# A block order at the start of two feed-forward phases, a third weight buffer and an earlier routing stage in an attention and mixture-of-experts kernel

## The chip, the cores and the metric

The kernel runs on one core of a Trainium2 chip. The metric is the device time of one execution in microseconds. The kernel before took 1055.02 us, the median of three runs (1054.81 to 1056.46).

## What is computed

Three layers follow each other. In the reference, cut to what matters:

```python
# 1 attention: 4 batches, 8 heads, 768 positions, head size 64; local window 96, 8 global positions
scores = q @ k^T / 8 + bias;  a = softmax(scores);  x = (a @ v) as 3072 tokens x 512
# 2 routing: all 3072 x 8 logits in falling order, an expert takes 384 tokens at most
logits = x @ w_gate
for idx in argsort(-logits.flatten()):
    tok, e = idx // 8, idx % 8
    if assigned[tok] < 0 and counts[e] < 384: assigned[tok] = e; counts[e] += 1
for e in range(8):
    out[mask] = relu(x[mask] @ w1[e]) @ w2[e]        # 512 -> 1024 -> 512
# 3 one dense layer for all tokens
out = (relu(out @ w_in) ** 2) @ w_out                # 512 -> 2048 -> 512
```

## The kernel before

After the attention, a router finds in eight stages which expert is full next and which 384 tokens it has. As soon as a stage is done, the 384 rows of that expert are gathered from memory (an indirect DMA from GpSimd, three of 128 rows), and TensorE runs two phases on them: phase A is the expert's own two matrices (`phase_a`), phase B the dense layer on the same rows (`phase_b`). The order is A and B of the first expert, A and B of the second, and so on (`SEQ`); experts are counted here from 0.

Every 32-bit matmul operand is held as a high half and a low half, and a product is three matmuls: high with high, high with low, low with high (`mm3`). ScalarE copies the high half, VectorE or GpSimd subtracts it for the low half. The rows' transposed operand x (or, in phase B, y) is `xy`: x[0] the high half, x[1] the low half, each of four pieces of 128 rows by 384 tokens, made piece by piece by `parts`.

Phase A goes over 8 row blocks f of 128 hidden units. A block's first product has 12 matmuls into one PSUM bank (`hg`), then `relu` makes the two halves of the result: ScalarE reads the bank first, VectorE reads it after that. Two blocks later 12 matmuls add the second product into four banks (`y`). Phase B goes over 16 row blocks in the same manner, but its `square` reads the bank once, with ScalarE's relu, and its second product (`outp`, 9 matmuls into three banks `o`) comes one block later. The `hg` banks are two, `pt0` and `pt1`, in turn; the transposes of the next expert's rows (`xpose`) use them too.

The weights of phase A are loaded per block (`loads`), and split by `splits`: two tiles of high halves `wh` by ScalarE (one for each product), two of low halves `wl` by GpSimd. The tiles of the first product have two buffers, so block f+2 is split when block f's matmuls have been issued. In the first expert, phase A's first block already sends its 8 matmuls with x[0] ahead of the 4 with x[1]. The weights of phase B stay on the chip; their second matrix is converted during the first expert (`conv`, with the buffers `ob`, of which two are called `cab0` and `cab1`).

A planner (`Sched`, with the costs in `take`) puts the generators' steps of all engines in one order by modelled times and priorities; a `yield` with a function waits until it is true. The routing stage `routing(1)` starts when the first expert's four x pieces are done. A stage has some preparing operations on VectorE, a transposition on TensorE, a search of eleven rounds on VectorE, and a closing part with short matmuls.

Of the kernel before, what the change touches and what calls it, by code (L numbers as in the profile page):

```python
# [6 lines left out]
FT = mybir.dt.float32  # L7
# [172 lines left out]
FR = mybir.dt.float32r  # L180
# [27 lines left out]
def tags(name, n):  # L208
    return tuple(f"{name}{i}" for i in range(n))
# [290 lines left out]
class Router:  # L500
# [110 lines left out]
    def stage(self, s, wp, ps, idx, eidx):  # L611
# [104 lines left out]
        else:  # L716
# [22 lines left out]
            yield "DVE"  # L739
            V.scalar_tensor_tensor(wv[:, 128:192], pv[:, 192:256], self.half[:, 1:2], wv[:, 128:192], op0=OP.mult, op1=OP.add)  # L740
            yield "DVE"
            for d in range(11):
                n, cur = (4, self.tw0) if d == 0 else (JW, thw)
                for j in range(1, n):
# [231 lines left out]
def ffn(tc, pools, router, ident, xd, wab, wov, wol, out, tail, wih, wil):  # L976
# [59 lines left out]
    def routing(s):  # L1036
        idx[s] = sb.tile([128, 3], I32, "idx", tags("idx", 8))
        eidx[s] = sb.tile([1, 1], I32, "eidx", tags("eidx", 8))

        if s == 1: yield lambda: parted["x", 0] == 4  # L1040
        for r in router.stage(s, wp, rps, idx[s], eidx[s]):
            if r == "e": known.add(s)
            elif r == "idx": done.add(s)
            elif r == "soon": soon.add(s)
            else: yield r
        if s + 1 < NE: S.add(routing(s+1), PR[s+1], -1)
    def first_gather():
# [25 lines left out]
    def splits():  # L1073
        for a in range(8*NE):
            yield lambda: a in raw
            w = raw.pop(a)
            W[a] = []
            for k in range(2):
                c = slice(k*512, k*512+512)
                yield lambda: n["ph"] > a - 2 if k == 0 else n["y"] > a - 4  # L1080
                hi = sb.tile([128, 512], FR, f"wh{k}", (tags("w", 2), tags("w", 7)[4:] + ("craw0",))[k])
                lo = sb.tile([128, 512], FR, f"wl{k}", (tags("w", 4)[2:], tags("w", 10)[7:] + ("craw1",))[k])
                yield ("ACT", [w[:, c]], [hi])
                ACT.copy(hi, w[:, c])
                yield first_gather
                yield ("POOL", [hi], [lo])
                G.tensor_tensor(lo, w[:, c], hi, op=OP.subtract)
                W[a] += [hi, lo]
            n["split"] += 1
    def loads_o():  # L1090
# [50 lines left out]
    def parts(kind, s, kc, v):  # L1141
        d = xy
        yield ("ACT", [v], [d[0][:, kc]])
        ACT.copy(d[0][:, kc], v)
        yield ("DVE", [d[0][:, kc]], [d[1][:, kc]])
        V.tensor_tensor(d[1][:, kc], v, d[0][:, kc], op=OP.subtract)
        parted[kind, s] += 1
        if kind == "y" and s not in kept: n["acc"] -= 1
    def xpose(s, kcs, slots):

        yield lambda: s in gathered
        p = {}
        for i, kc in enumerate(kcs):
            p[kc] = pp.tile([128, 384], FT, "xtp" + slots[i], (slots[i],))
        for k in range(3):
            yield ("PE", [xg[:, k]], [p[kcs[0]]])
            for kc in kcs:
                PE.transpose(p[kc][:, k*128:k*128+128], xg[:, k, kc*128:kc*128+128], ident)
        for kc in kcs: S.add(parts("x", s, kc, p[kc]), 0)
        if kcs[-1] == 3: xposed.add(s)  # L1160
    def mm3(o, sh, sl, mh, ml, first, last):
        yield ("PE", [sh, sl, mh, ml], [o])
        PE.matmul(o, sh, mh, start=first, stop=False)
        PE.matmul(o, sh, ml, start=False, stop=False)
        PE.matmul(o, sl, mh, start=False, stop=last)
    hq, gq = {}, {}
    def relu(a, ph):
        hh, hl = rot("hb", hb)
# [5 lines left out]
    def phase_a(s):  # L1174
        x, (nh, ns) = xy, follows["A", s]
        y = []
        yield lambda: parted["x", s] == 4
        for f in range(10):
            a = s*8 + f
            if f < 8:  # L1180
                yield lambda: len(W.get(a, ())) >= 2
# [59 lines left out]
    def rows_out(s, k, o, end):  # L1241
        ot = xg[:, k]
        e = "ACT" if k == 1 + end else "DVE"
        yield (e, [o], [ot])
        if e == "ACT": ACT.copy(ot, o)
        else: V.tensor_copy(ot, o)
        n["acc"] -= 1
        yield "POOL"
        G.memset(spacer, 0.0)
        st = G.indirect_dma_start(out=out, out_offset=bass.IndirectOffsetOnAxis(ap=idx[s][:, k:k+1], axis=0), in_=ot, in_offset=None)  # L1250
        for q in prevsc: tc.declare_no_dep(st.ins, q.ins, reason="other rows")
        prevsc.append(st)
        scattered[s] += 1
    def phase_b(s):
# [4 lines left out]
        def outp(f, ks=range(3)):  # L1259
# [11 lines left out]
            if 2 in ks:  # L1271
                n["out"] += 1
                WO.pop((s, f))
                gq.pop((s, f))
        for f in range(16):
            wh, wl = wih[f], wil[f]
            pg = pp.tile([128, 384], FT, "hg", tags("pt", 2))
            for kc in range(4):
# [3 lines left out]
            if f == 15:  # L1282
# [7 lines left out]
                for k in () if end else range(3):  # L1290
# [2 lines left out]
                        yield lambda: (s, 15) in gq  # L1293
                        yield from xpose(ns, (2, 3), ("pt0", "pt1"))
                    yield from outp(13+k)
            elif 1 <= f < 14:
                yield from outp(f-1)
    def main():

        yield lambda: 0 in done  # L1300
        warm = pp.tile([128, 512], FT, "warm", ("pt0",))
        for _ in range(NWARM):
            yield ("PE", [wih[0]], [warm])
            PE.matmul(warm, wih[0][:, 0:128], wih[0], start=True, stop=True)
        yield lambda: 0 in gathered
        yield from xpose(0, range(4), ("mi", "s0", "s1", "s2"))
        for h, s in seq:
            yield from (phase_a if h == "A" else phase_b)(s)
    def rows(g):
# [179 lines left out]
```

## Time and profile before

| | |
|---|---|
| median of three runs | 1055.02 us |
| profiled execution | 1056.06 us |
| its span, first to last instruction | 1054.3 us |
| TensorE busy (matmuls) | 1021.0 us, 97% |
| VectorE, ScalarE, GpSimd busy | 666.8, 497.2, 418.3 us |
| mean granted clock of TensorE | 0.985 |

The span is that of the profiled execution, which is one run; the median is of others. Matmuls are pipelined, so the length of one matmul in the profile (0.34 us for 384 columns) is longer than the time until the next one starts. Steps between starts are the better measure.

### The profile page before, as it was taken

The page shows a single profiled execution, that of the slowest core. Times are in us where ns is not written, and L with a number is a line of the kernel's source. Part 1 is how long each engine was busy: PE and PEld are TensorE (multiplying, and loading weights), DVE is VectorE, ACT ScalarE, POOL GpSimd, SP SyncE. Part 2 cuts the span into 40 slices and gives each one's busy share as a digit, 9 for nine tenths or more (in the row PEclk, how much of TensorE's full clock was granted, in tenths as well). Part 3 has the DMA queues.
Part 4 walks back from the last instruction along what each step waited for, and adds up shares of the span by engine and source line. Part 5 has one row for each costly group of instructions (what it writes and reads, how often), then busy time and mean ns, then how long its engine had stood idle before and what let it go on. Part 6 is the DMA issues. An engine that isn't in the chain of part 4 may idle for free.

```text
span 1054.3 us, 18941 instructions
## 1 busy us (share of the span) xinstructions
PE 1021.0 (97%) x6427; PEld 909.2 (86%) x6427; DVE 666.8 (63%) x2665; ACT 497.2 (47%) x1246; POOL 418.3 (40%) x458
## 2 busy tenths in 40 slices
PE   9999996899999999999999999999999999999997
PEld 6777775689889888998899889988998899999986
DVE  6999986799569857985797489559954111121111
ACT  8989995334433443334433433433343444333332
POOL 4756630653565143615261526252633272006001
PEclk9999997899999999999999999999999999999999
DMA  9989953553342133214231523242323243223121
GB/s 334 349 308 362 352 201 121 189 151 111 121 149 91 41 120 120 100 41 160 77 105 40 162 69 110 76 125 71 111 90 110 61 148 112 60 79 103 40 61 60
DMA packets 53041, 139.51 MB, mean 132 GB/s; under 512 B 6224, under 2 KB 6608, under 8 KB 52944
## 3 DMA queue, kind: packets, MB, share of 16 engines
q1 hardware_dynamic: 49104, 125.72, 36.1%
q0 software_dynamic: 3840, 12.59, 3.7%
q8 instruction: 50, 0.82, 0.3%
q14 instruction: 47, 0.39, 0.1%
HBM read 117.31 MB, written 20.97 MB: 131 GB/s over the span
## 4 chain that ended last, share of the span: by engine, by line
PE 78%; DVE 11%; issue 4%; ACT 3%; POOL 1%; DMA 1%; POOLq 0%; SPq 0%; DVEq 0%; ACTq 0%
PE hg L77 33%; PE o L77 23%; PE y L77 8%; DVE r_ge L77 4%; PE pt L321 3%; PE pxpx L337 3%; PE s L294 3%; ACT P L312 2%; PE r_ps L77 2%; DVE r_tc L77 1%; DVE r_th L77 1%; DVE r_pre L77 1%; PE natmi L383 1%; DMA c_xg<-xd,idx 1%; DVE r_fc L77 1%
## 5 line engine op out<-in xcount | busy, mean ns | idle before, releaser
L77 PE MATMUL hg<-c_XT,wi 128*128 128x384 f32 x1536 | 291.9, 338 | 2.2 <-DVE c_XT L77 2.2
L77 PEld LDWEIGHTS hg<-c_XT,wi 128*128 128x128 f32 x1536 | 270.4, 188 | 12.7 <-DVE c_XT L77 3.4
L77 ACT ACTIVATE c_gs<-hg 128x384 f32<-128x384 f32 x128 | 63.0, 492 | 281.5 <-PE hg L77 276.2
L77 POOL TENSOR_TENSOR wl<-c_T,wh 128x512 fp32r<-128x512 f32 x128 | 167.1, 1323 | 44.1 <-ACT wh L77 41.7
L77 DVE TENSOR_SCALAR_CACHE_REDUCE r_ge<-r_wv,r_th 128x192 bf16<-128x192 f32 x420 | 172.5, 411 | 11.7
L77 PE MATMUL hg<-c_XT,wh 128*128 128x384 f32 x512 | 132.0, 339 | 3.0 <-DVE c_XT L77 1.9
L77 ACT CAST wh<-c_T 128x512 fp32r<-128x512 f32 x128 | 75.1, 617 | 59.4 <-DMA c_T<-in_wab 57.7
L77 PEld LDWEIGHTS hg<-c_XT,wh 128*128 128x128 f32 x512 | 92.6, 188 | 6.0 <-DVE c_XT L77 3.7
L77 POOL DMA_INDIRECT out<-c_xg,idx x24 | 23.7, 986 | 183.6 <-DVE c_xg L77 169.0
L312 ACT ACTIVATE P<-ns,nm 128x232 f32<-128x232 f32 (+1 forms) x192 | 90.1, 475 | 13.6 <-DVE nm L304 13.2
L77 PE MATMUL hg<-c_XT,wl 128*128 128x384 f32 x256 | 87.1, 340 | 0.7
L77 POOL TENSOR_TENSOR c_k<-c_q,c_k 128x384 fp32r<-128x384 f32 x24 | 25.0, 1042 | 134.1 <-ACT c_k L77 114.3
L77 PE MATMUL o<-wol,c_k 128*128 128x512 f32 x192 | 76.4, 398 | 0.0
L77 ACT ACTIVATE c_q<-c_gs 128x384 f32<-128x384 f32 x128 | 67.2, 525 | 9.0 <-ACT c_gs L77 0.4
L304 DVE CUSTOM_DVE_ANT_0 ns<-s,T 128x232 f32<-128x232 f32 (+1 forms) x192 | 61.4, 375 | 9.0 <-PE s L294 4.0
L321 PE MATMUL pt<-ident,P 128*128 128x128 f32 x352 | 52.3, 283 | 2.6 <-ACT PT L326 2.3
L321 PEld LDWEIGHTS pt<-ident,P 128*128 128x128 f32 x352 | 37.3, 141 | 20.2 <-ACT PT L326 9.5
L77 PE MATMUL y<-c_k,wh 128*128 128x384 f32 x192 | 54.7, 338 | 0.0
L77 PEld LDWEIGHTS hg<-c_XT,wl 128*128 128x128 f32 x256 | 48.1, 188 | 3.4 <-POOL wl L77 3.3
L326 ACT COPY PT<-pt 128x512 f32<-128x512 f32 (+1 forms) x94 | 50.5, 537 | 0.3 <-PE pt L321 0.3
L77 POOL TENSOR_TENSOR c_v<-c_q,c_k 128x384 fp32r<-128x384 f32 x24 | 24.8, 1033 | 62.3 <-ACT c_k L77 48.7
L294 PE MATMUL s<-kr,qr 64*128 64x232 f32 (+1 forms) x384 | 48.6, 372 | 0.0
(304 smaller groups left out, 2087.9 us busy)
## 6 DMA issues: line engine op xcount, KB each, us to landing
c_T<-in_wab SPq DMA_DIRECT2D x64, 512.0 KB, 3.5
wol<-wol SPq DMA_DIRECT2D x128, 256.0 KB, 2.6
raw<-in_m SPq DMA_DIRECT2D x32, 512.0 KB, 7.9
vr<-in_v SPq DMA_DIRECT2D x16, 704.0 KB, 5.7
xd<-xn SPq DMA_DIRECT2D x24, 256.0 KB, 4.0
kr<-in_k SPq DMA_DIRECT2D x15, 404.0 KB, 7.3
qr<-in_q SPq DMA_DIRECT2D x15, 384.0 KB, 7.1
wov<-ct SPq DMA_DIRECT2D x16, 256.0 KB, 6.3
```

What stands on the lines that cost most here:

```text
L77: return f(*a, **k)
L294: PE.matmul(s[a][:, :n], qr[h, i*128:i*128+128], kr[h, c0:c0+n], start=True, stop=True)
L304: V.tensor_tensor_reduce(out=ns[:, a, :n], in0=s[a][:, :n], in1=tb, scale=-0.125, scalar=BIG, op0=OP.add, op1=OP.min, accum_out=nm[:, a:a+1])
L312: ACT.activation(P[:, a, :n], ns[:, a, :n], AF.Exp, bias=nm[:, a:a+1], scale=-1.0, accum_out=s)
L321: PE.transpose(pt[:, c, a], P[:, a, c*128:c*128+128], ident)
L326: copy(PT[:, :n], st[u][:, :n])
L337: PE.matmul(px[a*64:a*64+64], vr[:, max(2*i-1, 0)+c, a*64:a*64+64], PT[:, c, a], start=c == 0, stop=c == n-1)
L383: PE.transpose(GM[3][:, hp*128:hp*128+128], XT[b][:, hp, i*128:i*128+128], ident)
```

## The change

Eight edits, in the order of the diff. (1) A stage of the router yields a mark "search" ahead of its search. (2) `routing(1)` waits for the first expert's x there, no longer at its start. (3) `splits` has a third buffer (`cab0`, `cab1`) for the first product's weights from the second expert on; the first use of it waits until all 16 conversions are done. (4) The low halves of the first expert's blocks 0 and 1 are made by VectorE, without the wait for the first gather; all others by GpSimd as before. (5) `xpose` can put matmuls whose result is not used between the second and third row block; the first expert gets one of 512 columns. (6) `first_two` sends the 16 matmuls of blocks 0 and 1 with the high halves of x or y, then the 8 with the low halves; phase A of experts 1 to 7 and phase B of all use it. Phase B's second product of blocks 0, 1 and 2 moves one block later, and two stand at block 4. (7) The last copy of the last phase is split, half on ScalarE and half on VectorE. (8) The warm-up matmuls become a function.

```diff
@@ Router.stage
             yield "DVE"
+            yield "search"
             for d in range(11):
@@ routing
-        if s == 1: yield lambda: parted["x", 0] == 4
         for r in router.stage(s, wp, rps, idx[s], eidx[s]):
...
+            elif r == "search":
+                if s == 1: yield lambda: parted["x", 0] == 4
@@ splits
-                yield lambda: n["ph"] > a - 2 if k == 0 else n["y"] > a - 4
-                hi = sb.tile([128, 512], FR, f"wh{k}", (tags("w", 2), tags("w", 7)[4:] + ("craw0",))[k])
-                lo = sb.tile([128, 512], FR, f"wl{k}", (tags("w", 4)[2:], tags("w", 10)[7:] + ("craw1",))[k])
+                m = 2 if a < 8 else 3
+                yield lambda: n["ph"] > a - m and (a != 10 or len(freed) == 16) if k == 0 else n["y"] > a - 4
+                hi = sb.tile([128, 512], FR, f"wh{k}_{m}", (tags("w", 2) + ("cab0",)[:m-2], tags("w", 7)[4:] + ("craw0",))[k])
+                lo = sb.tile([128, 512], FR, f"wl{k}_{m}", (tags("w", 4)[2:] + ("cab1",)[:m-2], tags("w", 10)[7:] + ("craw1",))[k])
...
-                yield first_gather
-                yield ("POOL", [hi], [lo])
-                G.tensor_tensor(lo, w[:, c], hi, op=OP.subtract)
+                if a >= 2: yield first_gather
+                yield ("POOL" if a >= 2 else "DVE", [hi], [lo])
+                (G if a >= 2 else V).tensor_tensor(lo, w[:, c], hi, op=OP.subtract)
@@ xpose
+            if k == 1: yield from warm(w)
@@ new
+    def first_two(x, w):
+        p = [pp.tile([128, 384], FT, "hg", tags("pt", 2)) for _ in w]
+        for kc in range(4):
+            c = slice(kc*128, kc*128+128)
+            for o, (wh, wl) in zip(p, w):
+                yield ("PE", [wh[:, c], wl[:, c], x[0][:, kc]], [o])
+                PE.matmul(o, wh[:, c], x[0][:, kc], start=kc == 0, stop=False)
+                PE.matmul(o, wl[:, c], x[0][:, kc], start=False, stop=False)
+        for o, (wh, wl) in zip(p, w):
+            for kc in range(4):
+                c = slice(kc*128, kc*128+128)
+                yield ("PE", [x[1][:, kc]], [o])
+                PE.matmul(o, wh[:, c], x[1][:, kc], start=False, stop=kc == 3)
+        return p
@@ phase_a
-        for f in range(10):
+        if s > 0:
+            a = s*8
+            yield lambda: len(W.get(a, ())) >= 2 and len(W.get(a+1, ())) >= 2
+            p = yield from first_two(x, [W[a][:2], W[a+1][:2]])
+            for i in range(2):
+                n["ph"] += 1
+                S.add(relu(a+i, p[i]), 0)
+        for f in range(2 if s > 0 else 0, 10):
@@ rows_out
-        if e == "ACT": ACT.copy(ot, o)
+        if k == 1 + end == 2:
+            ACT.copy(ot[:, 0:256], o[:, 0:256])
+            V.tensor_copy(ot[:, 256:512], o[:, 256:512])
+        elif e == "ACT": ACT.copy(ot, o)
@@ phase_b
-        for f in range(16):
+        p = yield from first_two(y, [(wih[f], wil[f]) for f in range(2)])
+        for f in range(2): S.add(square(s, f, p[f]), 0)
+        for f in range(2, 16):
...
-            elif 1 <= f < 14:
-                yield from outp(f-1)
+            elif f < 14:
+                for g in (f-2,) if f < 4 else (2, 3) if f == 4 else (f-1,): yield from outp(g)
+    def warm(n, dt=FT):
+        o, w = pp.tile([128, 512], FT, "warm", ("pt0",)), wih[0].bitcast(dt)
+        for _ in range(n):
+            yield ("PE", [w], [o])
+            PE.matmul(o, w[:, 0:128], w, start=True, stop=True)
@@ main
-        yield from xpose(0, range(4), ("mi", "s0", "s1", "s2"))
+        yield from xpose(0, range(4), ("mi", "s0", "s1", "s2"), 1)
```

## Rows read from the trace of the kernel before

**Rows 1.** Busy time by window: length, engines with counts, clock, DMA share, GB/s

```profile
198.25:1047.50 849.25, 841.35 (x4526) 772.79 (x4526) 500.85 (x1972) 335.23 (x661) 319.82 (x298) 1.00 0.31 98
302.40:306.60 4.20, 4.20 (x14) 3.31 (x14) 2.64 (x6) 0.86 (x2) 2.26 (x3) 0.59 0.17 62
193.90:198.20 4.30, 2.46 (x17) 1.67 (x16) 0.16 (x1) 0.48 (x2) 4.28 (x5) 1.00 0.50 131
```

**Rows 2.** TensorE in order of time at second phases: start, length, operation, idle before

```profile
234.29 0.33 PE L77 MATMUL hg<-c_XT,wi 128*128 128x384 f32 x1
236.29 4.28 PE L77 MATMUL hg<-c_XT,wi 128*128 128x384 f32 x23 [1.67 <-DVE c_XT L77]
240.41 0.40 PE L77 MATMUL o<-c_k,c_q 128*128 128x512 f32 x1
...
345.77 0.34 PE L77 MATMUL hg<-c_XT,wi 128*128 128x384 f32 x1
...
350.57 0.40 PE L77 MATMUL o<-c_k,c_q 128*128 128x512 f32 x1
...
558.17 0.34 PE L77 MATMUL hg<-c_XT,wi 128*128 128x384 f32 x1
...
562.77 0.40 PE L77 MATMUL o<-c_k,c_q 128*128 128x512 f32 x1
...
980.19 4.36 PE L77 MATMUL hg<-c_XT,wi 128*128 128x384 f32 x24
984.38 0.40 PE L77 MATMUL o<-c_k,c_q 128*128 128x512 f32 x1
```

**Rows 3.** ScalarE in order of time, at four places

```profile
163.01 0.27 ACT L342 COPY xT<-pxpx 128x128 f32<-128x128 f32 x1 [1.55 <-DVE xT L342]
...
845.80 0.49 ACT L77 ACTIVATE c_q<-hg 128x384 fp32r<-128x384 f32 x1 [2.23 <-PE hg L77]
...
982.50 0.49 ACT L77 ACTIVATE c_gs<-hg 128x384 f32<-128x384 f32 x1 [1.63 <-PE hg L77]
...
1047.63 0.59 ACT L77 COPY c_xg<-o 128x512 f32<-128x512 f32 x1 [4.68 <-PE o L77]
```

**Rows 4.** TensorE's weight loads in order of time, first phase of expert 2

```profile
417.86 0.19 PEld L77 LDWEIGHTS hg<-c_XT,wh 128*128 128x128 f32 x1 [0.77 <-DVE c_XT L77]
...
422.81 0.19 PEld L77 LDWEIGHTS hg<-c_XT,wl 128*128 128x128 f32 x1 [0.44 <-POOL wl L77]
```

**Rows 5.** TensorE in order of time, first phases of experts 2 and 6

```profile
417.86 0.45 PE L77 MATMUL hg<-c_XT,wh 128*128 128x384 f32 x1 [0.33 <-DVE c_XT L77]
...
424.66 0.34 PE L77 MATMUL y<-c_q,wh 128*128 128x384 f32 x1
...
843.49 0.34 PE L77 MATMUL hg<-c_XT,wh 128*128 128x384 f32 x1
...
850.09 0.34 PE L77 MATMUL y<-c_q,wh 128*128 128x384 f32 x1
```

**Rows 6.** VectorE in order of time, at five places

```profile
161.71 0.42 DVE L359 COPY gs<-gm 128x256 f32<-128x256 f32 x1 [0.35 <-PE gm L356]
...
200.10 0.34 DVE L77 TENSOR_REDUCE r_m<-L 128x24 f32<-128x192 f32 x1
...
204.79 2.67 DVE L77 TENSOR_TENSOR r_t<-r_t,L 128x128 f32<-128x128 f32 x2
...
271.98 0.85 DVE L77 TENSOR_TENSOR r_Tw<-r_dg,r_pre 128x1 int32<-128x1 int32 x1
...
846.40 0.56 DVE L77 SCALAR_TENSOR_TENSOR c_q<-hg,c_q 128x384 fp32r<-128x384 f32 x1 [2.02 <-ACT c_q L77]
```

**Rows 7.** TensorE in order of time, around stage 1's end and expert 1's transposes

```profile
274.08 0.27 PE L77 MATMUL r_ps<-ident,r_Tw 128*128 128x128 f32 x1
...
295.00 4.35 PE L77 MATMUL hg<-c_XT,wi 128*128 128x384 f32 x24
...
302.22 0.33 PE L77 MATMUL xtpmi<-ident,c_xg 128*128 128x128 f32 x1 [0.91 <-DMA c_xg<-xd,idx]
```

More of the change, by code (lines that the diff above doesn't have):

```diff
@@ L1148, in parts, with xpose @@
         if kind == "y" and s not in kept: n["acc"] -= 1
-    def xpose(s, kcs, slots):
+    def xpose(s, kcs, slots, w=0):
         yield lambda: s in gathered
@@ L1295, in phase_b @@
                     yield from outp(13+k)
-            elif 1 <= f < 14:
-                yield from outp(f-1)
+            elif f < 14:
[5 more added lines that the diff above has]
+            PE.matmul(o, w[:, 0:128], w, start=True, stop=True)
     def main():
         yield lambda: 0 in done
[L1301 to L1304, printed above, removed]
+        yield from warm(NWARM, FR)
         yield lambda: 0 in gathered
-        yield from xpose(0, range(4), ("mi", "s0", "s1", "s2"))
+        yield from xpose(0, range(4), ("mi", "s0", "s1", "s2"), 1)
         for h, s in seq:
```

## Prediction

> **What bounds the kernel now.** I read the busy shares by window first, then TensorE's order of time around each start of a phase, then the engines that it waits for. From the first expert matmul to the last, TensorE is busy for nearly all of the stretch and the clock is full in it [rows 1]; what a reordering can win is therefore the sum of a few gaps, and only some of them are at the edited places. The reader is to see three kinds. A second phase that starts undisturbed sends its first 24 matmuls in 4.19 us, 0.175 each (980.19 to 984.38 in expert 7) [rows 2]; the first expert's takes 6.12, because the low halves of y (VectorE) come late. Block 2 of each first phase waits for its low weights (GpSimd). And expert 1's gathered rows come late, with a stretch of half clock behind the wait [rows 1].
>
> **Starts of the second phase.** The new order sends 16 matmuls that need only the high halves before the first that needs a low half. 16 x 0.175 = 2.8 us of cover; the wait was 1.67 us for expert 0 [rows 2]. Lost before: 6.12 - 4.19 = 1.93 for expert 0; 4.80 - 4.19 = 0.61 for expert 1, 0.41 for expert 3 (562.77 - 558.17), some 0.24 between them for expert 2; nothing from expert 4 on. Gain 3.2 us.
>
> What is late next is a PSUM bank. Both blocks hold the two banks pt0 and pt1, and block 2 takes pt0 again. Block 0's last matmul now comes only 4 matmuls, 0.70 us, before block 2 (it was a whole block, 2.1 us). In the second phase the bank is free when ScalarE's relu has read it: in expert 7, 12 matmuls from 980.19 end at 982.29, the relu starts at 982.50 and takes 0.49 [rows 3], 0.70 after the end. So block 2 just misses its start. A weight load that stood behind such a wait began together with its matmul [rows 4, 5], so about half of its 0.19 us is exposed, 0.1 (estimate). With the wake-up I take 0.15 a phase, 8 phases: 1.2 us lost. Bounds: nothing, if the bank is in time; 0.6 each, if ScalarE has just begun another copy of the length of the last row of [rows 3]: 4.8.
>
> **Starts of the first phase, experts 1 to 7.** Here the old block 0 already sent its 8 high-half matmuls first, and no matmul waited for a low half of x; the wait at expert 2's start is for bank pt0, which VectorE's subtraction still reads [rows 5]. The new order can win nothing there. It needs pt1 at its third matmul as well; the second subtraction follows the first by about the length of two matmuls, so I cost that at nothing.
>
> The third buffer lets block 2's weights be split during the phase before. Won is the wait for the low weights [rows 4]. From the start of block 0 to the first y matmul are 36 matmuls, 6.31 us; expert 6 took 6.60, so 0.29; expert 2 took 6.80, of which 0.1 is its start, so 0.39 [rows 5]. Experts 1, 6, 7 at 0.29 and 2 to 5 at 0.39: gain 2.4 us. The two extra GpSimd subtractions move into a phase in which GpSimd has room, and cost nothing; had they to stay (expert 1 needs all 16 converted matrices first), block 2 waits for the bank anyway.
>
> Lost is the bank again, and here it is longer: the bank is free only after relu on ScalarE and then the low half on VectorE. In expert 6 block 0's 12 matmuls end at 843.49 + 12 x 0.1757 = 845.60; relu starts at 845.80 [rows 3], the subtraction starts at 846.40 and takes 0.56 [rows 6]: 1.36 after the end. Block 2 now wants the bank 0.70 after the end. Wait 0.66, plus the exposed load and the wake-up: 0.85 a phase, 7 phases, 6.0 us lost. Bounds: 0.66 each, 4.6; one more VectorE instruction of 0.56 in front, 1.41 each, 9.9.
>
> **A rule weighed on this.** The trace shows a weight load standing with its waiting matmul [rows 4]. The Trainium skill, "TensorE: Matmul & The Clock Gate", section "Architectural detail", says that TensorE's queue can pull weight loads ahead of matmuls in flight; by that rule the 0.1 exposed at each of the 15 places is hidden and the sum is 1.5 us lower; by the row it is paid. I go by the row, and keep the other as a rival.
>
> **First expert and second stage.** From 193.9 to 198.2 VectorE is busy for only 0.16 us, and GpSimd for 4.28 [rows 1]: it is GpSimd's four subtractions of the weights of blocks 0 and 1. On VectorE they cost about 0.56 x 512/384 = 0.75 each, 3.0 us in all, under that idle time; without that cover they would delay the low halves of x by as much. GpSimd gains nothing, since block 2's weights in the first expert still wait for the buffer. The spare matmul of 512 columns between the second and third transposes sits in the same window, in which TensorE idles for 4.30 - 2.46 = 1.84 us in two gaps; four times a 128-column transpose of 0.33 [rows 7] is 1.3, so it costs between nothing and some 0.4. I take nothing.
>
> The second stage's preparation began at 200.10, when x was done, and the last of its large additions starts at 204.79 and takes 2.67 for two [rows 6]. Moved forward, at best its first 1.3 us fit before x's subtractions, and its slow part escapes GpSimd: some 2.5 us earlier. But the four subtractions and the tail of stage 0 come first on the same VectorE, and stage 0's last step passes through TensorE between or behind the third transposes: at worst nothing is won.
>
> Worth to the path: expert 1's transposes. The 24 matmuls from 295.00 end at 299.19; the third row block's transposes would follow at 299.7 and came at 302.22 [rows 7], 2.5 us lost. Then, behind these idle times, 4.20 us ran at a mean granted clock of 0.59, touching the lower level of 1.2 GHz [rows 1]: 4.20 x 0.41 = 1.7 lost. Bounds 0 and 4.2. I take 0.8, a third of the wait and none of the clock.
>
> Against it: expert 0's second phase runs 1.8 us earlier, but the stage's search is VectorE's and does not. It ends at 271.98 + 0.85 = 272.83 [rows 6]; TensorE takes the result at 274.08 [rows 7], slack 1.25. TensorE would wait 0.5 there.
>
> **End.** The last copy is split between ScalarE and VectorE. Two engines that read one bank are put behind each other: ScalarE's copy at 163.01 waited for VectorE's of the same bank [rows 3]. Half on VectorE is 0.42, as its 256-column copy at 161.71 [rows 6]; half on ScalarE some 0.37, between its 0.27 for 128 columns and 0.59 for 512 [rows 3]. One after the other 0.79 against 0.59: 0.2 lost; side by side it would be 0.2 won. The moved order of the output matmuls has the same count, and their operands are ready earlier relative to use: nothing.
>
> **Sum.** -3.2 - 2.4 + 6.0 + 1.2 + 0.5 - 0.8 + 0.2 = +1.5 us. The profiled execution took 1056.06 us (span 1054.3), 1.04 above the median of 1055.02; all terms are differences, so I add to the median: 1056.5. What a measurement can tell from no change is about 0.2%, 2.1 us, so this is no change: 1052.9 to 1057.1.
>
> **Rivals.**
> - Faster: the second stage leads. If its search starts 2.5 us earlier, the gathered rows are in time, the clock stays up, the 0.5 is not paid: 1.5 - 3.4 - 0.5 = -2.4, 1052.6; with the bank at its lower bound 1051.2. For it: the idle VectorE before x. Against: the four subtractions put there, and stage 0's last step through TensorE. It decides once the rows come about 2 us earlier relative to TensorE.
> - Slower: the bank costs its upper bound in the first phase, because VectorE is inside its search in experts 1 to 5: +3.9, 1060.4. Against it: in expert 6 the subtraction followed the relu by 0.1 us, though no search ran beside it.
> - The early preparation does nothing: stage 0's last step falls behind the third transposes, and the stage starts behind x as before. Then the 0.8 is missing: 1057.3.
> - The queue's rule: weight loads hidden behind the wait, 1.5 less, 1055.0.
>
> **Chances.** Forecast 0.33 (of it 0.24 within 0.2%, 0.09 slower); second stage leads 0.27 (0.20 faster, 0.07 within); bank at its bound 0.15 (slower); preparation does nothing 0.20 (half within, half slower); queue's rule 0.05 (within). Together faster 0.20, within 0.46, slower 0.34. The range goes from between the two values of the first rival to just under the second: 1052.0 to 1060.0.
>
> **What would show it.** In the new trace block 2 of the first phases of experts 1 to 7 should wait for VectorE's low half, 0.6 to 1 us, and no longer for GpSimd's low weights; in second phases for ScalarE's relu, 0.2 or less. Expert 0's second phase should start without the 1.67 us wait. Stage 1's first reduction should stand before or behind x's subtractions at about 198 to 200; expert 1's third transposes at about 300 if the rival holds. I am wrong if block 2 starts without a wait (then faster by up to 6), or if the half-clock stretch goes.

## The result and the profile after

The changed kernel took 1065.76 us, the median of four runs (1063.40 to 1066.54), against 1055.27 for the kernel before, now the median of four. The ratio on record is 1.0083, interval 1.0070 to 1.0095, or 9 us; the two medians differ by 10.5. The time lies outside the predicted range of 1052.0 to 1060.0. A second measurement gave 1.0086 (1.0068 to 1.0104).

The profiled execution took 1063.40 us with a span of 1061.6, 7.3 us more than the span before. Where these 7.3 us come from is read from TensorE's first matmul of each phase. It divides the span into the start of the first expert (198.25 us before, 200.25 after: +2.0), its phase A (36.04, 36.29: +0.25), the seven later phases A (239.95 in all, 242.66: +2.7), the phases B of experts 0 to 6 (505.95, 507.92: +2.0, of which expert 0's is 1.2 shorter and the others 3.2 longer), and the end (+0.4). This execution was the fastest of its four, so it holds less than the whole loss; the second profile, below, shows more of it.

Windows of the changed kernel, in the columns of [rows 1]: from the first expert matmul to the last, the stretch ahead of the first one, and the stretch of half clock at expert 1's rows.

```profile
200.25:1055.20 854.95, 843.06 (x4526) 772.62 (x4526) 527.06 (x1974) 334.24 (x662) 318.60 (x296) 1.00 0.31 96
193.90:198.20 4.30, 3.38 (x14) 1.95 (x13) 4.16 (x11) 0.00 (x0) 2.29 (x2) 0.87 0.93 323
304.30:308.00 3.70, 3.70 (x11) 2.89 (x10) 3.63 (x6) 1.19 (x3) 3.70 (x4) 0.54 0.33 91
```

In the first line VectorE is busy 527.06 us where [rows 1] has 500.85, with two instructions more: its instructions got longer. In the second VectorE is busy for 4.16 of 4.30 us, where the prediction had counted on 0.16, and the DMA share is 0.93 instead of 0.50. The half clock stayed (0.54).

TensorE in order of time, at the first phase A, the first phase B, one wait for the router, the phase A of expert 6 and the last phase B; then its weight loads at that phase B.

```profile
199.36 0.33 PE L77 MATMUL xtpmi<-ident,c_xg 128*128 128x128 f32 x1 [1.13 <-DMA c_xg<-xd,idx]
...
199.85 0.19 PE L77 MATMUL r_ps<-ones,r_Ab 128*128 128x1 bf16 x2
200.25 0.45 PE L77 MATMUL hg<-c_XT,wh 128*128 128x384 f32 x1 [0.21 <-ACT c_XT L77]
...
236.54 6.93 PE L77 MATMUL hg<-c_XT,wi 128*128 128x384 f32 x36
243.31 0.40 PE L77 MATMUL o<-c_k,c_q 128*128 128x512 f32 x1
...
712.56 0.20 PE L77 MATMUL r_ps<-ones,r_Ab 128*128 128x1 bf16 x2 [1.20 <-DVE r_Ab L77]
...
849.34 0.34 PE L77 MATMUL hg<-c_XT,wh 128*128 128x384 f32 x1
...
854.23 0.62 PE L77 MATMUL hg<-c_XT,wh 128*128 128x384 f32 x2 [0.55 <-DVE c_q L77]
...
856.45 0.52 PE L77 MATMUL y<-c_q,wh 128*128 128x384 f32 x2
```

```profile
991.36 2.06 PEld L77 LDWEIGHTS hg<-c_XT,wi 128*128 128x128 f32 x12 [0.20 <-ACT c_gs L77]
```

The wait of 1.67 us at the first phase B [rows 2] is gone: its first 36 matmuls stand in one row without an idle time. In phase A (expert 6) block 2 waits 0.55 us for VectorE's low half; its 36 matmuls take 7.11 us (849.34 to 856.45) where the low weights let them take 6.60 before [rows 5]. In phase B the weight load of block 2 waits 0.20 for ScalarE. The third gathered rows come at 199.36, 2.0 us later than in the kernel before:

```profile
197.36 0.33 PE L77 MATMUL xtpmi<-ident,c_xg 128*128 128x128 f32 x1 [0.86 <-DMA c_xg<-xd,idx]
```

The router's short product (`r_ps`) now stands behind them.

VectorE in order of time, the first row from the kernel before, the others from the changed one: in the first expert's start, at one router stage's end, and at the last copy.

```profile
191.60 0.36 DVE L77 TENSOR_TENSOR L<-L,r_gt 128x192 f32<-128x192 f32 x1
...
191.28 0.68 DVE L77 TENSOR_TENSOR wl<-c_T,wh 128x512 fp32r<-128x512 f32 x1
...
194.69 1.75 DVE L77 TENSOR_TENSOR L<-L,r_gt 128x192 f32<-128x192 f32 x1
...
198.08 0.29 DVE L77 CAST r_Ab<-r_As 128x256 bf16<-128x256 f32 x1
...
202.17 0.35 DVE L77 TENSOR_REDUCE r_m<-L 128x24 f32<-128x192 f32 x1
...
398.88 0.79 DVE L77 TENSOR_TENSOR idx<-cum 128x3 int32<-128x3 f32 x1
...
1055.13 0.42 DVE L77 COPY c_xg<-o 128x256 f32<-128x256 f32 x1 [1.10 <-ACT c_xg L77]
```

The four subtractions stand inside stage 0's tail, one of whose operations takes 1.75 us (0.36 before). The tail ends with `r_Ab` at 198.37, 193.89 before, and the second stage's first reduction comes at 202.17, behind x, where [rows 6] has it at 200.10.

GpSimd in order of time at the same router stage, the first row again from the kernel before. There the gather of expert 2's rows is issued 0.27 us after the index (`idx`, 397.02); now it is issued at 404.01, 4.3 us after the index was there (399.67), behind two subtractions, one of them of weights, and 1.8 us in which GpSimd idled.

```profile
397.29 0.99 POOL L77 DMA_INDIRECT c_xg<-xd,idx  x1 [0.29 <-DVE r_t L77]
...
401.44 1.15 POOL L77 TENSOR_TENSOR c_q<-c_q,c_q 128x384 fp32r<-128x384 f32 x1 [1.79 <-issue]
402.56 1.29 POOL L77 TENSOR_TENSOR wl<-c_T,wh 128x512 fp32r<-128x512 f32 x1
404.01 0.99 POOL L77 DMA_INDIRECT c_xg<-xd,idx  x1 [0.15 <-issue]
```

ScalarE's half of the last copy:

```profile
1054.72 0.37 ACT L77 COPY c_xg<-o 128x256 f32<-128x256 f32 x1 [4.68 <-PE o L77]
```

VectorE's half waited for it: 0.83 us for both instead of 0.59.

### The profile page after: what moved, and what is told of

It reads as the page before. It is cut to its first block, busy times and chain, and to the rows that moved or that the text cites. A ratio compares the mean times of both kernels' runs of the same rounds, so it can differ in the third digit from the quotient of the medians.

```text
span 1061.6 us, 18924 instructions
## 1 busy us (share of the span) xinstructions
PE 1024.5 (97%) x6429; PEld 910.2 (86%) x6429; DVE 696.3 (66%) x2670; ACT 495.5 (47%) x1246; POOL 414.2 (39%) x454
## 4 chain that ended last, share of the span: by engine, by line
PE 81%; DVE 11%; ACT 4%; issue 2%; DMA 1%; POOL 1%; POOLq 0%; DVEq 0%; ACTq 0%
PE hg L77 34%; PE o L77 22%; PE y L77 12%; PE pt L321 3%; PE pxpx L337 3%; DVE r_ge L77 3%; PE s L294 3%; ACT P L312 3%; PE r_ps L77 2%; DMA c_xg<-xd,idx 1%; ACT PT L326 1%; PE natmi L383 1%; DVE c_q L77 1%; DVE r_tc L77 1%; DVE r_pre L77 1%
## 5 line engine op out<-in xcount | busy, mean ns | idle before, releaser
L77 POOL TENSOR_TENSOR wl<-c_T,wh 128x512 fp32r<-128x512 f32 x124 | 163.4, 1330 | 66.5 <-ACT wh L77 66.4
L77 PEld LDWEIGHTS hg<-c_XT,wh 128*128 128x128 f32 x512 | 92.5, 188 | 10.5 <-DVE c_q L77 6.0
L337 PE MATMUL pxpx<-PT,vr 128*64 128x128 f32 x680 | 47.5, 280 | 0.0
```

Of the source, the lines that this page charges most:

```text
L77: return f(*a, **k)
L337: PE.matmul(px[a*64:a*64+64], vr[:, max(2*i-1, 0)+c, a*64:a*64+64], PT[:, c, a], start=c == 0, stop=c == n-1)
```

## The experiments

Two theories went through the runs, with their rivals. T1: the change's parts cost separately, VectorE's subtractions at the start, the third buffer through GpSimd's work beside VectorE's routing, and the bank in phase A; its rival R: the planner's new order made the router late. T3 sharpened the second part: a VectorE operation that meets GpSimd's stands, so what GpSimd does beside the router's closing part decides; against it R2 (the router sets everything, or the parts overlap) and R4 (the buffer itself). Each ratio is to the kernel before, timed on the same chip; the kernels were spread over several chips. The last three columns (us) come from one profiled execution of each kernel, up to some 3 us from the median of its runs, so they need not add up to the ratio; and up to 1.6 us of the first matmul's differences are there already when the first gather is issued (190.66 to 192.31).

| kernel | ratio (interval) | first matmul | phases A 1 to 7 | phases B 0 to 6 |
|---|---|---|---|---|
| before | 1 | 198.25 | 239.95 | 505.95 |
| changed, second profile | 1.0086 (1.0068 to 1.0104) | 200.19 | 242.68 | 510.16 |
| low weights on GpSimd again | 1.0026 (1.0017 to 1.0036) | 199.17 | 243.34 | 504.26 |
| no third buffer | 1.0189 (1.0172 to 1.0205) | 202.01 | 258.80 | 501.17 |
| old phase A | 1.0023 (1.0011 to 1.0035) | 200.19 | 236.63 | 509.63 |
| old gate of the second stage | 1.0086 (1.0070 to 1.0101) | 201.67 | 242.67 | 507.02 |
| phase B alone | 0.9968 (0.9955 to 0.9981) | 198.87 | 239.75 | 504.89 |
| phase B and third buffer | 1.0003 (0.9994 to 1.0012) | 198.28 | 236.64 | 508.98 |
| early gate alone | 1.0002 (0.9988 to 1.0016) | 198.22 | 240.83 | 505.74 |
| GpSimd's weights and old phase A | 0.9989 (0.9980 to 0.9998) | 198.29 | 236.76 | 505.64 |
| loads held | 1.0083 (1.0068 to 1.0098) | 202.07 | 242.74 | 507.56 |
| phase B alone, splits held | 1.0144 (1.0126 to 1.0162) | 198.22 | 239.39 | 519.91 |
| phase B, third buffer, splits held | 1.0097 (1.0081 to 1.0112) | 199.59 | 236.78 | 521.20 |
| subtractions on both engines | 1.0106 (1.0090 to 1.0121) | 201.07 | 242.84 | 507.77 |
| phase B, third buffer, block 2 on VectorE | 0.9945 (0.9931 to 0.9958) | 198.98 | 236.78 | 504.74 |
| the same, blocks 0 to 2 | 0.9989 (0.9980 to 0.9998) | 198.90 | 237.44 | 507.74 |

**One part undone.** First the low weights on GpSimd:

```diff
-                if a >= 2: yield first_gather
-                yield ("POOL" if a >= 2 else "DVE", [hi], [lo])
-                (G if a >= 2 else V).tensor_tensor(lo, w[:, c], hi, op=OP.subtract)
+                yield first_gather
+                yield ("POOL", [hi], [lo])
+                G.tensor_tensor(lo, w[:, c], hi, op=OP.subtract)
```

> The low halves of the first expert's blocks 0 and 1 go back to GpSimd, behind the first gather; all else stays as in the changed kernel. Theory T1: these four subtractions on VectorE, and the earlier loads that they allow, cost the 2.0 us at the first expert's start and kept the second stage behind x. Then the third row block's transposes come back from 199.36 to about 197.4, the first phase A starts near 198.3 instead of 200.25, and the time falls by 2.0 us; if the second stage's first reduction now comes before x's subtractions (before 198), expert 1's gather comes earlier too and the time falls by 3 to 5 us in all. Theory R: the start of the second stage stays where the planner puts it (behind 200) and only the 2.0 us go.

It won 0.57 to 0.60 per cent against the changed kernel, some 6 us by the ratios (4.8 between the medians of this kernel and of the second measurement), T1's larger case or a little more; R fell. The second stage starts at 197.55 and expert 1's gather is issued at 293.76 instead of 297.04. The spans of this profile and of the second one of the changed kernel differ by 4.8 us too: the first matmul comes 1.0 earlier, phases B of experts 0 and 1 are 2.1 and 3.4 shorter, phases A 2.1 longer. The indices of experts 1 and 2 come 3.2 and 5.7 us earlier, and the waits for their rows, 0.92 and 1.88 us, are gone. So most of the price of VectorE's low weights is paid in the phases B of experts 0 and 1, through a late router. The early preparation has its own price, seen in TensorE's and VectorE's order of time in this kernel:

```profile
203.18 2.19 PE L77 MATMUL hg<-c_XT,wh 128*128 128x384 f32 x6 [2.25 <-DVE c_XT L77]
```

```profile
197.55 0.34 DVE L77 TENSOR_REDUCE r_m<-L 128x24 f32<-128x192 f32 x1
197.93 3.96 DVE L77 TENSOR_TENSOR r_t<-L,r_m 128x192 f32<-128x192 f32 x1
```

A preparing operation of 0.36 us stands for 3.96 while GpSimd subtracts weights (from 195.46 on), x's low halves wait behind it, and TensorE for them. Of the 2.1 us that the first phase B wins, the first phase A loses 1.6 against the changed kernel's first profile.

Then the third buffer (`m = 2`):

```diff
-                m = 2 if a < 8 else 3
+                m = 2
```

> The third buffer is taken out, so block 2's weights are split inside phase A again; all else stays. Theory T1: the two GpSimd subtractions that the third buffer moved into phase B lengthen VectorE's small operations at the end of each routing stage, so the stages' period grew from about 98.7 to 102.4 us and TensorE waits for the router in phases B. Then the period falls back to about 99, VectorE's busy time from 696 towards 670, the waits for the router's products of 0.4 to 1.2 us go, and the time falls by 2.5 to 4 us; phase A keeps its length, since block 2 waits for the bank about as long as it would for its low weights. Theory R: the period grew because of the order that the planner made of the new blocks and of the router's steps; then the period stays above 102 and the time changes by less than 1 us, or grows by the 0.3 a phase that the low weights cost.

Both theories fell on time: 1.0 per cent slower, not faster. T1's half on phases B came, 6.8 us shorter; its phase A, which was to keep its length, did not, and the stages' period (99.3 to 102.0 us) fell only in part. TensorE at expert 1's phase A:

```profile
319.37 0.62 PE L77 MATMUL hg<-c_XT,wh 128*128 128x384 f32 x2 [1.09 <-ACT wh L77]
320.75 0.44 PE L77 MATMUL hg<-c_XT,wl 128*128 128x384 f32 x1 [0.76 <-POOL wl L77]
```

With blocks 0 and 1 together, the buffer comes free only after both, so the split of block 2 begins some 2 us later (ScalarE's part 4.8 to 5.0 us after the phase's first matmul, 2.7 to 2.8 in the kernel before), and a phase A takes 1.6 to 3.4 us more than in the changed kernel. The two edits need each other.

Phase A in the old order:

```diff
-        if s > 0:
+        if False:
...
-        for f in range(2 if s > 0 else 0, 10):
+        for f in range(10):
```

> Phase A of experts 1 to 7 goes back to the old order of its blocks; phase B keeps the two blocks together, and the third buffer stays. Theory T1: the wait of block 2 for its bank, 0.55 us and 0.82 with the load behind it, goes in seven phases, and the wait for the low weights does not come back: 5.7 us less. Every phase A of experts 1 to 7 should take about 33.9 to 34.0 us from its first matmul to phase B's, against 34.5 to 34.9 now. Theory R: something else makes phase A longer, and the phases stay above 34.3; less than 2.5 us.

T1 held: phases A at 33.8 us each, 6.0 us less in all, and 0.63 per cent of time. The old gate:

```diff
+        if s == 1: yield lambda: parted["x", 0] == 4
         for r in router.stage(s, wp, rps, idx[s], eidx[s]):
...
-                if s == 1: yield lambda: parted["x", 0] == 4
+                pass
```

> The second stage waits for the first expert's x at its start again, no longer ahead of its search; all else stays. Theory T1: the second stage started behind x anyway, so nothing changes: within 0.5 us, the stages' period stays near 102.4. Theory R: moving the wait let the planner place the stage's steps in an order that made all later stages late; then the period falls back to about 99 and the time falls by some 3 us.

T1 held, no difference in time. R fell: the gate did not make the stages late.

**One part alone.** These three begin from the kernel before. Phase B has only this part of the diff:

```diff
+        p = yield from first_two(y, [(wih[f], wil[f]) for f in range(2)])
+        for f in range(2): S.add(square(s, f, p[f]), 0)
+        for f in range(2, 16):
...
+                for g in (f-2,) if f < 4 else (2, 3) if f == 4 else (f-1,): yield from outp(g)
```

> The kernel before with one part of the change: phase B's first two blocks together, with the later order of its second product; two buffers, the old phase A, GpSimd for all low weights, the old gate of the second stage, no spare matmul, no split at the end. Theory T1: the starts win 3.2 us, the bank costs 1.2 at most: 1 to 3 us faster than before, and VectorE keeps its 667 us. Theory R2: the new order of phase B alone brings VectorE's routing operations beside GpSimd's, as every changed kernel so far has shown (686 to 699 us busy): then VectorE is above 680 us and the time is that of before or slower.

It is 0.32 per cent faster, 3.4 us, although VectorE's busy time rose to 681.1 us. T1's time held; its VectorE, at 667 us, did not. R2's lengthening is there, and its time fell: the longer VectorE did not decide. The two profiled executions hold 1.1 us of the gain in phases B; the rest is not located. Next, the third buffer added:

```diff
+                m = 2 if a < 8 else 3
```

> As the kernel with phase B's edit alone, and with the third buffer; phase A in the old order. Theory T1: against phase B's edit alone another 2.4 us, since block 2 of phase A no longer waits for its low weights and its bank is free: phase A of experts 1 to 7 takes 33.8 us, and the time is 3 to 5 us under before. Theory R2: the split weights move GpSimd's work beside VectorE's routing, which gives the gain back: between 0 and 3 us slower than phase B's edit alone.

Each half is right. Phases A took 3.1 us less, and phases B took 4.1 more; the kernel is 0.35 per cent, 3.7 us, slower than without the buffer, a little past R2's 3 us. (The two profiled spans differ by 0.5 us only: this one is among the fastest of its runs, the other the slowest.) Around the router's stages it shows where (TensorE, GpSimd, VectorE):

```profile
409.67 0.33 PE L77 MATMUL xtpmi<-ident,c_xg 128*128 128x128 f32 x1 [2.07 <-DMA c_xg<-xd,idx]
...
707.83 0.20 PE L77 MATMUL r_ps<-ones,r_Ab 128*128 128x1 bf16 x2 [1.20 <-DVE r_Ab L77]
```

```profile
599.61 2.86 POOL L77 TENSOR_TENSOR wl<-c_T,wh 128x512 fp32r<-128x512 f32 x2
602.63 0.99 POOL L77 DMA_INDIRECT c_xg<-xd,idx  x1 [0.16 <-DVE r_tie L77]
```

```profile
599.98 1.34 DVE L77 TENSOR_TENSOR A<-A,r_t 128x192 f32<-128x192 f32 x1
601.24 1.28 DVE L77 TENSOR_TENSOR r_tie<-r_M,r_ac 128x24 f32<-128x24 bf16 x1
```

Beside GpSimd's two subtractions, VectorE's operations take 1.34 and 1.28 us, which take 0.36 and 0.17 where they meet nothing, and the gather stands behind the subtractions. Without the buffer GpSimd has four subtractions of weights in the routing stage's closing part, with it six. With it TensorE has four waits that it does not have without: the 2.07 us for expert 2's rows, and 0.60, 1.20 and 0.39 for `r_Ab` at 606, 708 and 809 us. They make 4.3 us, beside the 4.1 that phases B grew, though not phase by phase.

> The kernel before with one part of the change: the second stage's gate stands ahead of its search, so its preparation may run before x's subtractions. Theory T1: with GpSimd doing the low weights, stage 0's last step comes before the third transposes and the preparation starts before 198; expert 1's gather is earlier by 1 to 3 us and the time 1 to 3 us shorter. Theory R2: the preparation takes VectorE's time from x's low halves, so that phase A of the first expert waits for them (2.25 us behind VectorE in the kernel with only the low weights undone): nothing won, within 0.5 us of before, or up to 2 us slower.

The early gate alone (the diff's "search" edit) starts the preparation at 196.69, and wins nothing: the first phase A becomes 1.1 us longer, and expert 1's gather is issued at 296.81, not earlier than 296.07 before. R2 held.

The changed kernel with the low weights on GpSimd and the old phase A, both diffs above:

> The changed kernel with two edits undone: GpSimd makes the first expert's low weights, and phase A keeps its old order; phase B's two blocks, the third buffer, the early gate, the spare matmul and the split copy stay. Theory T1: the two costs are separate, 0.57 and 0.60 per cent, and add: some 1.17 per cent below the changed kernel, 0.996 to 0.998 of before. Theory R2: both act through the same thing, how VectorE's routing operations fall beside GpSimd's, and overlap: 1.000 to 1.002 of before.

0.9989 is between the two expectations. Against this kernel, both blocks together in phase A cost 0.37 per cent (1.0026), VectorE's low weights 0.34 (1.0023), both 0.97. That is 0.26 more than the sum of the two, about as much as the intervals allow: the costs do not overlap, and whether they only add or make each other worse is not shown.

**Why the start is late, and why the buffer costs.**

> The changed kernel again, unedited, beside the others on one chip: 1.007 to 1.010 of before. Its single profile of 1063.4 us was the fastest of its first four runs; this one shows whether the phases' times of that profile are typical.

The phases agree with the first profile within 0.7 us but for expert 1's phase B, 75.10 us instead of 72.18. TensorE, and a window behind it, in this second profile:

```profile
413.10 0.43 PE L77 MATMUL xtpmi<-ident,c_xg 128*128 128x128 f32 x1 [1.88 <-DMA c_xg<-xd,idx]
```

```profile
413.10:417.00 3.90, 3.90 (x11) 3.16 (x12) 2.78 (x11) 1.03 (x3) 0.30 (x2) 0.56 0.00 0
```

Expert 2's rows come so late that TensorE idles 1.88 us, and then 3.9 us run at a granted clock of 0.56. This one phase is 2.9 us longer; the two profiled spans differ by 2.3.

```diff
-            yield lambda: n["split"] > a - 2
+            yield lambda: n["split"] > a - 2 and (a < 2 or first_gather())
```

> The changed kernel, VectorE still making the first expert's low weights, but the loads of its third and later blocks wait for the first gather, as they did when GpSimd made them. Theory T1: the third gathered rows were late because these loads ran beside the gather (341 GB/s against 175 in the six microseconds before the first phase): the third transposes come back to 197.4 to 198.3 and the first phase A starts 1 to 2 us earlier; the second stage still starts behind x, since VectorE's four subtractions still stand in stage 0's tail. 1.5 to 2.5 us less than the changed kernel. Theory R3: it is VectorE's time alone, not the transfers; then the third transposes stay at 199.4 and the time stays.

Inconclusive: the loads didn't move. They were issued at 193.62 and 195.09 us, beside the gather's third part (194.73); from 193.9 to 198.2 the DMA rate was 319 GB/s, 323 without the edit, and the rows were late again (201.09).

```diff
-... (a != 10 or len(freed) == 16) if k == 0 else ...
+... (a != 10 or len(freed) == 16) and (a < 8 or a // 8 in gathered) if k == 0 else ...
```

> Phase B's edit alone, and the splits of the next expert's weights wait until its rows' gather has been issued, so GpSimd has four subtractions less beside the router's closing part. Theory T3: each routing operation of VectorE that meets a GpSimd operation takes 0.4 to 1.1 us instead of 0.17 to 0.36; with the four subtractions away VectorE is busy some 5 us less than with phase B's edit alone (681), the stages' period shrinks below 98.5 us, but TensorE hardly waits for the router there, so the time changes by less than 1 us. Theory R2: the router sets TensorE's order throughout, and the time falls by 2 us or more.

> As the kernel with phase B's edit and the third buffer, which was 0.35 per cent slower than without the buffer, with the next expert's splits held until its rows' gather has been issued. Theory T3: the loss came from six subtractions beside the router's closing part, by slower VectorE operations and by a gather that stands behind two subtractions (2.9 us from index to issue instead of 0.3): the stages' period falls from 101 to 98.5 us or less, phase A keeps 33.8 us, and the time is 2 to 4 us under phase B's edit alone (0.993 to 0.995 of before). Theory R4: the third buffer itself, its loads or its bank order, makes phase B longer: phases B of experts 1 to 5 stay near 73 us and the time stays at 1.000.

Both theories fell on time: 1.8 and 0.9 per cent slower than without the edit. Held until the gather, the splits run in one bunch behind it, as TensorE, GpSimd and VectorE show in the kernel with the third buffer:

```profile
407.60 0.21 PE L77 MATMUL r_ps<-ones,r_Ab 128*128 128x1 bf16 x2 [4.71 <-DVE r_Ab L77]
```

```profile
400.53 1.03 POOL L77 TENSOR_TENSOR c_q<-c_q,c_q 128x384 fp32r<-128x384 f32 x1
401.50 2.52 POOL L77 TENSOR_TENSOR wl<-c_T,wh 128x512 fp32r<-128x512 f32 x2
403.97 0.99 POOL L77 TENSOR_TENSOR c_k<-c_q,c_k 128x384 fp32r<-128x384 f32 x1
404.92 2.47 POOL L77 TENSOR_TENSOR wl<-c_T,wh 128x512 fp32r<-128x512 f32 x2
```

```profile
400.27 7.27 DVE L77 CAST r_Ab<-r_As 128x256 bf16<-128x256 f32 x1
```

A cast that takes 0.29 us alone [after, at 198.08] stood 7.27, until GpSimd's run ended at 407.39, and TensorE waited 4.71 for it. Without the buffer the same shows at 504 and 608 us, with waits of 4.17 and 4.10 for `r_Ab`. It is the mechanism of T3 at its clearest; the expected time was wrong because the edit moved the collision to a worse place.

```diff
-                if a >= 2: yield first_gather
-                yield ("POOL" if a >= 2 else "DVE", [hi], [lo])
-                (G if a >= 2 else V).tensor_tensor(lo, w[:, c], hi, op=OP.subtract)
+                if a < 2:
+                    yield ("DVE", [hi], [lo])
+                    V.tensor_tensor(lo, w[:, c], hi, op=OP.subtract)
                 yield first_gather
                 yield ("POOL", [hi], [lo])
                 G.tensor_tensor(lo, w[:, c], hi, op=OP.subtract)
```

> The changed kernel with GpSimd making the first expert's low weights of blocks 0 and 1 again, and VectorE making the same four as well, ahead of it, for nothing; the loads stay as late as GpSimd sets them. If VectorE's time is the cause of the 5 us that these subtractions cost, the second stage's first reduction falls back behind x (above 200) and the time stays near the changed kernel, 1.006 to 1.009 of before. If the earlier loads beside the gather are the cause, the third transposes stay near 198 and the time near the kernel with GpSimd alone, 1.002 to 1.004.

The time, 1.0106, is past VectorE's case and far from the other. TensorE, a window and VectorE:

```profile
197.75 0.33 PE L77 MATMUL xtpmi<-ident,c_xg 128*128 128x128 f32 x1
...
201.00 0.20 PE L77 MATMUL r_ps<-ones,r_Ab 128*128 128x1 bf16 x2 [2.60 <-DVE r_Ab L77]
```

```profile
193.90:198.20 4.30, 3.89 (x19) 2.48 (x17) 4.27 (x4) 0.08 (x1) 4.24 (x4) 0.86 0.50 143
```

```profile
194.51 4.21 DVE L77 COPY closed<-r_est 128x8 f32<-128x8 f32 x1
```

With the loads late again (143 GB/s, not 323) the third rows are in time, at 197.75 without a wait. So the earlier loads made them late. All kernels agree: from the issue of the gather's third part to its transposes it is 5.1 to 7.1 us in the six with the earlier loads, and 3.6 to 3.8 in the other eleven. But stage 0's tail, pushed by 2 us into GpSimd's subtractions, lost 4.21 us in one small copy, and TensorE waited 2.60 for it. So either can hold the start: in the changed kernel the rows came after `r_Ab` (199.36 and 198.37), here they came before it. How the 6 us divide between the late rows, VectorE's own 2.7 us and a collision isn't settled by this run, whose collision the changed kernel does not have.

```diff
-                yield ("POOL", [hi], [lo])
-                G.tensor_tensor(lo, w[:, c], hi, op=OP.subtract)
+                v = a >= 8 and a % 8 == 2
+                yield ("DVE" if v else "POOL", [hi], [lo])
+                (V if v else G).tensor_tensor(lo, w[:, c], hi, op=OP.subtract)
```

> Phase B's edit and the third buffer, with the low weights of block 2 of each later expert made by VectorE in 0.68 us each instead of GpSimd in 1.3. T3: GpSimd's run beside the router's closing part is as short as without the third buffer, VectorE pays 1.4 us a stage for it: the stages' period goes from 101 to 99 or 100 us, phase A keeps its 33.8 us, and the time is 1 to 3 us under phase B's edit alone, 0.994 to 0.996 of before. R4: the buffer's own place or its loads make phase B longer; then the time stays at 1.000.

T3 held in the time, 0.9945, some 5.8 us under the kernel before and faster than phase B alone and than phase B with the buffer. Phases A are as short as with the buffer (236.78), phases B as short as without it (504.74). GpSimd and VectorE at expert 2's gather:

```profile
398.53 0.99 POOL L77 DMA_INDIRECT c_xg<-xd,idx  x1 [1.72 <-DVE r_t L77]
```

```profile
398.10 0.15 DVE L77 TENSOR_TENSOR idx<-cum 128x3 int32<-128x3 f32 x1
```

The gather follows the index by 0.28 us (4.46 with all weights on GpSimd). But the stages' period didn't go back: 100.5 to 105.2 us. The four waits of 4.3 us are gone; what is left, 0.96 for `r_Ab` and 0.94 for rows in the first phase B, phase B alone has too (0.92 and 0.97). Not the period, then, but which waits TensorE meets (for the gathered rows and for `r_Ab`) carries the cost.

> The same with the low weights of blocks 0, 1 and 2 of each later expert on VectorE, so that GpSimd makes none beside the router's closing part. T3: VectorE's routing operations lose their long cases there, six subtractions cost 4.1 us a stage in their place: the stages' period is 98 to 101 us and the time 0.993 to 0.997 of before. R4: 1.000 or more; also if VectorE's own 4.1 us take the place of what GpSimd cost.

Here `v` is `a >= 8 and a % 8 < 3`. 0.9989 lies between the two: VectorE's six subtractions a stage give back most of it. The profile shows nearly all of the loss at one place, expert 0's phase B, 78.79 us, where TensorE waits 2.77 us for the first rows and then runs at half clock; the other phases B are as short as with one block on VectorE. So more work there is worse on either engine, by these two runs.

## Why the prediction was wrong

The prediction went wrong in two terms that it took as nothing. None of its own signs of being wrong came: block 2 waited and the half clock stayed; the loss lay elsewhere. In parts, from the kernel before, each step one of the runs above: phase B -3.4 us, third buffer +3.7, early gate with spare matmul and split copy -1.5, both blocks together in phase A +3.9, VectorE's low weights +6.3; +9 in all (per cent by 10.55). The last two depend on their order: the other way round they are 3.6 for the low weights and 6.6 for the blocks.

- **Starts of phase B: the mechanism right.** Predicted -3.2 for the starts, +1.2 for the bank and +0.5 for the router, -1.5; alone it gave -3.4 with an interval of 1.4 on either side, so somewhat more. From expert 1 on the first 36 matmuls took 6.45 us where 6.29 are undisturbed, so the bank cost 0.16 a phase for the 0.15 predicted. The wake-up in that 0.15, and in phase A's 0.85, stands in no row. The router's wait was 0.92.
- **The bank in phase A: right.** Predicted +6.0. Phases A are 6.0 us shorter in the old order (242.66 against 236.63 us), and block 2 waited for VectorE's low half as described. Its upper bound, and the rule that weight loads hide behind the wait, did not come true: the load's wait is in the trace.
- **Third buffer: the gain right, its price missed.** Phases A gave 3.1 us for 2.4 predicted, and phases B took it back. The step that failed reads: "The two extra GpSimd subtractions move into a phase in which GpSimd has room, and cost nothing". GpSimd had room; VectorE beside it did not, and neither had the gather behind it. With one of the three blocks' subtractions on VectorE the price went (0.9945). The same sentence's "had they to stay [...] block 2 waits for the bank anyway" failed too: without the buffer block 2 waited for its weights, 1.09 and 0.76 us.
- **VectorE's low weights: missed, 3.6 to 6.3 us.** The second step that failed: "3.0 us in all, under that idle time" was read from a window that starts at 193.9. The subtractions began at 191.28, ahead of stage 0's tail, and took its place. I had named that order, but only as the loss of the early preparation, 0.8 us, and not priced what is late next: `r_Ab` by 4.5 us, the stage's start by 2, the rows of experts 1 and 2. And I had not asked what a freed buffer triggers: the next 512 KB loads ran beside the first gather, at 323 instead of 131 GB/s, and made its third rows 2.0 us late.
- **Early preparation: its rival came true.** The stage started behind x in the changed kernel (202.17), and early preparation did next to nothing alone.
- **End: right**, 0.2 predicted, 0.25 from the copy's start to the last scatter's issue (1.11 us, 0.86 before).

What connects both failures is a rate between two engines that [rows 6] already showed, two additions of 2.67 us, and that I used only there. Over five of the traces, VectorE operations with an input from the PSUM banks and the reductions (0.35 us) kept their time beside GpSimd; many of those with two inputs from SBUF, the casts and copies from SBUF and the small operations with a constant (TENSOR_SCALAR) took up to 1.75 us beside one GpSimd subtraction, and up to 7.27 beside a run of them. The `r_fc` group, 66 in number, went from a mean of 256 ns to this in the changed kernel:

```profile
L77 DVE CUSTOM_DVE_ANT_0 r_fc<-r_G,one 128x7 f32<-128x7 f32 (+1 forms) x66 | 24.2, 367 | 2.2
```

The Trainium skill says the same in "SBUF — State Buffer", section "Who interferes with whom": an operation of VectorE with two SBUF inputs, or a copy or cast in its two-port mode, contends with GpSimd for a shared pair of ports, and whoever holds it blocks the other. The traces agree in which kinds of operation suffer, and the 7.27 us shows a waiting operation that was not let in between GpSimd's consecutive ones.

## What to carry to other kernels

Before work is moved to "an engine with room", list which operations of its neighbour stand in the same stretch: room on GpSimd can be paid by VectorE, and then by whoever waits for VectorE or for a gather in GpSimd's queue. When an engine takes over a step, read from which moment the step is ready, not when the engine is idle, and what the buffer that it frees will load. Two edits that share a buffer are priced together: here the change without its third buffer was 1.9 per cent slower than the kernel before, and the third buffer without them won only once its extra work stood on the right engine.

## What the runs showed of the hardware

A VectorE cast of 0.29 us stood 7.27 us beside six GpSimd operations in a row, a copy of 0.17 stood 4.21 beside three, a subtraction of 0.36 stood 3.96 beside a run of four; reductions (0.35) and subtractions that read PSUM (0.56) were not touched. The transposes of a gather's third rows came 3.6 to 3.8 us after its issue, and 5.1 to 7.1 where loads of 512 KB ran beside it. Two engines that copy halves of one PSUM bank went one after the other (0.37, then 0.42 us). An idle time of 1.88 us of TensorE was followed by 3.9 us at a mean granted clock of 0.56, most of it at the lower level of 1.2 GHz.
